# Clustered attention and two expert layers: a flag row for queries without keys, and one maximum over two PSUM banks in the first batch

## The chip, the core and the metric

One core of one Trainium2 chip. The metric is the device time of one execution in microseconds (us); the figure for a kernel is the median of its runs.

## The reference

Three stages follow each other. Attention: 2 batches, 8 heads, 768 positions, 64 columns. Each query and each key goes to the nearest of 16 centroids of its head, and a query sees only the keys of its own cluster:

```python
mask = q_assign[:, :, :, None] == k_assign[:, :, None, :]
scores = np.where(mask, scale * np.matmul(q, k.transpose(0, 1, 3, 2)), -1000000000.0)
attn = np.exp(scores - np.max(scores, axis=-1, keepdims=True))
attn = attn / (np.sum(attn, axis=-1, keepdims=True) + 1e-09)
return np.matmul(attn, v)
```

A query whose cluster holds no key has the same score everywhere, so its output is the mean of all values. The result, 1536 rows of 512, goes through a layer `s * relu(x @ w_in)**2 + b` times `w_out` (512 to 2048 to 512), and then through a layer of 8 experts of which each row uses the one with the largest gate.

## The kernel before, in words

A head is packed and transposed first (`prep1`, `prep2`). For each position `pk2` holds 128 columns in f16: 64 of the key (index 0) or the query (index 1), 16 of the one-hot cluster times a large number, then column 80, and zeros behind it. Column 80 is a constant on the key's side, and on the query's side it takes the query's negative maximum, so that a product of the packed rows gives a masked score with the maximum taken off. `prep2` also sums all values of the head in `vsp` (line 225) and keeps their mean in `vm` (line 227), on all partitions.

A unit is one head and one half of its queries: 3 chunks of 128, so that there are 32 units, 16 for each batch. `unit_max` (line 230) makes the maxima of a unit: for each chunk two matmuls of 384 keys into one PSUM bank each (line 239) and a reduce for each of the two (line 242), and behind the six a small reduce that joins the halves (line 248). The maxima go into column 80 (line 249), and the unit's packed queries are transposed into `qb`. After the second unit of a head an ACTIVATE makes a flag for each query whose maximum shows that it has no key (line 255).

`unit` (line 258) goes over 6 chunks of keys: two matmuls into `st` (lines 278 and 280), exponentials in f32 (`p`, line 283) and in half the cases in f16 too (`ph`, line 288, with the rest `pl` from POOL, line 291), and three chunks later their product with the values into `pv` (line 270), whose first column is the sum of the weights. Then VectorE makes the reciprocal and `x3` (lines 299 to 304), replaces the rows of flagged queries by `vm` with a COPY_PREDICATED (line 306), and ScalarE and POOL write `xp` in two parts (lines 309, 310).

The loop over heads runs `unit` of a head with `unit_max` of the next head, `prep2` of the one after that and `prep1` of the third laid in between, and from the ninth head on also steps of the second layer (`moe1`) for the first batch. Chunks of `w_in` and `w_out` are split into f16 pairs on the way (lines 324 to 333; 6 of them at the start, then in heads 5 and 7 to 11). This is the order of the program; within it a planner sets the order on each engine from a simulated timeline, and engines then run in order.

PSUM has eight banks. Before, two belong to `mm`, one to `aux`, two to `st`, two to `sm` and one to `pv`. In the first batch `mm` is free of the second layer, and the kernel uses it twice: for one of the six `sm` tiles of a unit, and for the `pv` of each second unit:

```python
sm = (mm.tile([P, HT], F32, name="sm", tag="mm") if n and c == 1 and i < H else
      sm_p.tile([P, HT], F32, name="sm"))
...
pv = (mm.tile([P, HC, D + 1], F32, name="pv", tag="mm") if i < H and qh else pv_p.tile([P, HC, D + 1], F32, name="pv"))
```

In the second batch all `pv` tiles come from the one bank of `pv_p`.

Of the kernel before, what the change touches and what calls it, by code (L numbers as in the profile page):

```python
# [26 lines left out]
BIGM = 32768.0  # L27
OOB = 1.0e6
# [15 lines left out]
def tile_kernel(ctx: ExitStack, tc, q, k, v, centroids, w_in, w_out, s, b, w_gate, w1, w2, out, dbg=None):  # L44
# [28 lines left out]
    mm = ctx.enter_context(tc.tile_pool(name="mm", bufs=2, space=PSUM))  # L73
# [7 lines left out]
    tpa = a0.enter_context(tc.tile_pool(name="tpa", bufs=4))  # L81
    at = ExitStack()
# [13 lines left out]
    sm_p = right("sm_p", 2, space=PSUM)  # L96
# [12 lines left out]
    def tpool(i):  # L109
        return tpa if i < H else tp  # L110

    def transpose(i, dst, src, pool=None):

        if i not in PE_T:
            nc.sync.dma_start_transpose(out=dst, in_=src.rearrange("p n x -> p (n x)"))
            return
        n0 = 2 * HC
        for g in range(0, src.shape[1], n0):
            nn = min(n0, src.shape[1] - g)
            odd = g // n0 % 2  # L120
            p, name = ((st_p, "st"), (sm_p, "sm"))[odd] if pool is None else pool
            ps = p.tile([P, n0, P], F16, name=name)
            for n in range(nn):
                nc.tensor.transpose(out=ps[:, n], in_=src[:, g + n], identity=ident)
            (nc.vector.tensor_copy if odd else nc.scalar.copy)(out=dst[:, g:g + nn], in_=ps[:, 0:nn])
# [34 lines left out]
    def iota(shape, pattern, base, mult, name):  # L160
# [10 lines left out]
    nc.gpsimd.memset(nokey, -BIGM * BIGM / 2)  # L171
# [5 lines left out]
                            compare_op=ALU.is_equal, fill=0.0)  # L177

# [6 lines left out]
    def pk2_clear(eng, i):  # L185
        eng.memset(pk2s[i][:, :, :, 64:128], 0.0)
        eng.memset(pk2s[i][:, 0, :, 64 + C], BIGM)

# [3 lines left out]
    def prep2(i):  # L192
# [33 lines left out]
        vm = tmp.tile([P, D], F32, name="vm", bufs=3)  # L226
        nc.scalar.activation(out=vm, in_=vsp, func=AF.Copy, scale=SX / S)
        h.update(pk2=pk2, tk2=tk2, qb={}, vm=vm)

    def unit_max(i, qh):  # L230
# [3 lines left out]
        mxt = small.tile([P, HC, 2], F32, name="mxt")  # L234
        for c in range(HC):
            for n in range(2):
                sm = (mm.tile([P, HT], F32, name="sm", tag="mm") if n and c == 1 and i < H else
                      sm_p.tile([P, HT], F32, name="sm"))
                nc.tensor.matmul(out=sm, lhsT=tk2[0:64 + C, 1, c0 + c, :],  # L239
                                 rhs=tk2[0:64 + C, 0, n * HC:(n + 1) * HC, :].rearrange("p c x -> p (c x)"),  # L240
                                 start=True, stop=True)
                nc.vector.tensor_reduce(out=mxt[:, c, n:n + 1], in_=sm, axis=AX.X, op=ALU.max)  # L242
                if (c, n) != (HC - 1, 1):
                    yield
        if not qh:
            h["mm1"] = small.tile([P, 2, HC], F32, name="mm1")
        mm1 = h["mm1"][:, qh]
        nc.vector.tensor_reduce(out=mm1, in_=mxt, axis=AX.X, op=ALU.max)
        st8[f"c{i}{qh}"] = nc.scalar.activation(out=pk2[:, 1, c0:c0 + HC, 64 + C], in_=mm1, func=AF.Copy, scale=-1.0 / BIGM)
        qb = tpool(i).tile([P, HC, P], F16, name="qb")  # L250
        transpose(i, qb, pk2[:, 1, c0:c0 + HC, :])
        h["qb"][qh] = qb
        if qh:
            h["flag"] = small.tile([P, 2, HC], F32, name="flag")
            nc.scalar.activation(out=h["flag"], in_=h["mm1"], func=AF.Relu, scale=-1.0, bias=nokey)
        yield

    def unit(i, qh, xp):
# [4 lines left out]
        pv = (mm.tile([P, HC, D + 1], F32, name="pv", tag="mm") if i < H and qh else pv_p.tile([P, HC, D + 1], F32, name="pv"))  # L263
# [12 lines left out]
        for kc in range(NC):  # L276
# [18 lines left out]
            yield  # L295
        for x in late:
            weigh(*x)
# [8 lines left out]
        nc.vector.copy_predicated(out=x3, mask=h["flag"][:, qh].bitcast(I32).unsqueeze(2).broadcast_to([P, HC, D]),  # L306
                                  data=h["vm"].unsqueeze(1).broadcast_to([P, HC, D]))
# [235 lines left out]
    for i in range(NH):  # L543
# [23 lines left out]
        if i == H - 1:  # L567
            a0.close()
            wop = ctx.enter_context(tc.tile_pool(name="wop", bufs=1, reuse_waits="tile"))
# [324 lines left out]
```

## Time and profile before

| | |
|---|---|
| median of 3 runs | 737.85 us (734.92 to 738.41) |
| the profiled execution's own time | 740.1 us |
| its span, first to last instruction | 738.4 us |
| mean granted clock of TensorE | 0.965 |
| busy: TensorE, VectorE, ScalarE, POOL | 89%, 71%, 59%, 40% |
| reduces of scores (line 242) | 192, mean 546 ns |
| COPY_PREDICATED (line 306) | 32, 21.8 us, mean 683 ns |
| products with the values (line 270), f16 | 1296, mean 195 ns |

A busy share is an average over stages: the first batch of attention ends at about 182 us, the second at about 415, the second layer at about 550, and the experts take the rest. Matmuls overlap in a pipeline, so the time from one's start to the next one's start is shorter than its duration; the same holds, by less, for VectorE.

### The profile page before, as it was taken

To read this page: it belongs to the slowest core of one execution; us is meant where nothing else is said; L and a number is where in the kernel's file an instruction comes from. 1 tells how busy PE (TensorE), PEld (TensorE's weight loads), DVE (VectorE), ACT (ScalarE), POOL (GpSimd) and SP (SyncE) were. 2 spreads that over 40 slices of the span, in tenths; PEclk is the share of its full clock that TensorE was granted. 3 is DMA by queue.
4 is the path that set the end of the run, shared out by engine and by line. 5 is a ranking of instruction groups with operands and counts; after the bars stand their busy time and mean duration, and the time that the engine had idled before them with its cause. 6 is when DMAs were issued, how large, how long until landed. Compare 5 with 4: busy or idle time off the path is not lost. (4 is left out here: it accounts for less than half of the span.)

```text
span 738.4 us, 16238 instructions
## 1 busy us (share of the span) xinstructions
PE 654.7 (89%) x6261; PEld 426.1 (58%) x6261; DVE 525.0 (71%) x1109; ACT 436.2 (59%) x897; POOL 293.5 (40%) x336
## 2 busy tenths in 40 slices
PE   2487888898877889999999999999999999998884
PEld 2255666676544545666655654565485776675651
DVE  7999798776899976588832661377844768777672
ACT  6477676777676745567734450156514568667562
POOL 6448576656666564644433300020013234331001
PEclk9998689999899999999999999999999999999898
DMA  8967666662563604430113400038933588789821
GB/s 235 185 158 154 146 169 145 154 133 54 141 158 95 150 25 99 107 70 7 34 13 67 85 15 1 15 110 260 373 101 100 127 270 270 163 270 255 258 101 52
DMA packets 122963, 98.33 MB, mean 133 GB/s; under 512 B 98812, under 2 KB 104956, under 8 KB 120576
## 3 DMA queue, kind: packets, MB, share of 16 engines
q1 hardware_dynamic: 112784, 65.64, 36.5%
q10 hardware_dynamic: 6576, 22.06, 9.4%
q0 software_dynamic: 3520, 9.54, 3.8%
q8 instruction: 51, 0.84, 0.5%
q14 instruction: 32, 0.26, 0.1%
HBM read 85.05 MB, written 7.39 MB: 125 GB/s over the span
## 5 line engine op out<-in xcount | busy, mean ns | idle before, releaser
L291 POOL TENSOR_TENSOR pl<-p,ph 128x384 f16<-128x384 f32 x128 | 128.4, 1011 | 116.4 <-ACT ph L288 58.7
L435 PE MATMUL ps<-xt,wi 128*128 128x384 f16 x768 | 135.3, 330 | 5.7 <-DMA xt<-xp 4.1
L449 PE MATMUL py<-wo,g 128*128 128x512 f16 x576 | 132.2, 382 | 0.0
L283 ACT ACTIVATE p<-st 128x384 f32<-128x384 f32 x192 | 94.1, 491 | 52.5 <-PE st L280 41.8
L242 DVE TENSOR_REDUCE mxt<-sm 128x1 f32<-128x384 f32 x192 | 102.3, 546 | 25.1 <-PE sm L239 24.5
L435 PEld LDWEIGHTS <-wi 128*128 128x128 f16 x768 | 74.5, 99 | 56.2 <-issue 10.4
L449 PEld LDWEIGHTS <-g 128*128 128x128 f16 x576 | 55.2, 98 | 64.0 <-issue 3.7
L239 PE MATMUL sm<-tk 80*128 80x384 f16 x192 | 64.5, 363 | 17.1 <-DVE mxt L242 11.9
L278 PE MATMUL st<-tk 128*128 128x384 f16 x192 | 65.6, 342 | 7.4 <-ACT ph L288 4.6
L288 ACT ACTIVATE ph<-st 128x384 f16<-128x384 f32 x144 | 70.9, 492 | 1.1 <-PE pv L270 1.1
L679 POOL DMA_INDIRECT out<-o,oid x16 | 26.9, 1682 | 103.4 <-ACT o L678 94.6
L280 PE MATMUL st<-qb,tk 128*128 128x384 f16 x192 | 65.8, 343 | 0.0
L673 PEld LDWEIGHTS <-ht 128*128 128x128 f16 x384 | 36.8, 98 | 44.5 <-issue 3.3
L441 ACT ACTIVATE g<-r,b 128x384 f16<-128x384 f32 x64 | 39.4, 618 | 37.1 <-DVE r L440 36.8
L442 DVE SCALAR_TENSOR_TENSOR g<-r,b,g 128x384 f16<-128x384 f32 x64 | 44.8, 701 | 21.3 <-ACT g L441 21.3
L270 PEld LDWEIGHTS <-ph 128*128 128x128 f16 x864 | 45.0, 99 | 20.9 <-issue 4.2
L270 PE MATMUL pv<-v,ph 128*128 128x65 f16 x864 | 52.0, 195 | 5.4 <-ACT ph L288 3.2
L516 POOL DMA_INDIRECT yreg<-yp,posi x12 | 12.8, 1069 | 106.6 <-DVE posi L502 86.1
L599 DVE SCALAR_TENSOR_TENSOR wa<-stg,wa 128x1024 f16<-128x1024 f32 x40 | 46.8, 1218 | 7.7 <-ACT wa L598 7.6
L659 PE MATMUL hps<-x2t,wa 128*128 128x128 f16 x768 | 45.7, 219 | 3.8 <-DVE wa L599 1.5
L659 PEld LDWEIGHTS <-wa 128*128 128x128 f16 x768 | 43.7, 98 | 6.8 <-issue 2.0
L440 DVE SCALAR_TENSOR_TENSOR r<-r,s 128x384 f32<-128x384 f32 x64 | 43.4, 678 | 4.2 <-ACT r L438 4.0
(216 smaller groups left out, 1248.0 us busy)
## 6 DMA issues: line engine op xcount, KB each, us to landing
stg<-in_moe_w SPq DMA_DIRECT2D x44, 1024.0 KB
raw<-in_moe_w_out ACTq DMA_DIRECT2D x16, 512.0 KB
stg<-in_moe_w ACTq DMA_DIRECT2D x8, 1024.0 KB
raw<-in_moe_w_in ACTq DMA_DIRECT2D x10, 512.0 KB
kqv<-in_k SPq DMA_DIRECT2D x16, 192.0 KB
kqv<-in_q SPq DMA_DIRECT2D x16, 192.0 KB
kqv<-in_v SPq DMA_DIRECT2D x16, 192.0 KB
raw<-in_moe_w_in SPq DMA_DIRECT2D x6, 512.0 KB
```

Of the source, the lines that this page charges most:

```text
L239: nc.tensor.matmul(out=sm, lhsT=tk2[0:64 + C, 1, c0 + c, :], rhs=tk2[0:64 + C, 0, n * HC:(n + 1) * HC, :].rearrange("p c x -> p (c x)"), s ...
L242: nc.vector.tensor_reduce(out=mxt[:, c, n:n + 1], in_=sm, axis=AX.X, op=ALU.max)
L270: nc.tensor.matmul(out=pv[:, c, :], lhsT=p[:, c * P:(c + 1) * P], rhs=w, start=first[0], stop=(kc == NC - 1 and c == HC - 1 and p is parts ...
L278: nc.tensor.matmul(out=st.rearrange("p (c x) -> p c x", c=HC), lhsT=tk1[:, kc, 0, :], rhs=tk1[:, c0:c0 + HC, 1, :], start=True, stop=False)
L280: nc.tensor.matmul(out=st, lhsT=tk2[:, 0, kc, :], rhs=qb.rearrange("p c x -> p (c x)"), start=False, stop=True)
L283: nc.scalar.activation(out=p32, in_=st, func=AF.Exp, scale=1.0 / 8.0)
L288: nc.scalar.activation(out=ph, in_=st, func=AF.Exp, scale=1.0 / 8.0)
L291: eng.tensor_tensor(out=pl, in0=p32, in1=ph, op=ALU.subtract)
L435: nc.tensor.matmul(out=ps, lhsT=wi[:, a, kk, f * P:(f + 1) * P], rhs=xt[:, c, kk], start=(kk == 0 and n == 0), stop=(kk == KD - 1 and n == 2))
L449: st8["py"] = nc.tensor.matmul(out=ps, lhsT=g[:, a, f, c * P:(c + 1) * P], rhs=wo[:, w, f], start=(f == 0 and n == 0), stop=(f == KF - 1 a ...
L599: nc.vector.scalar_tensor_tensor(out=lo[:, a:z], in0=stg[i][:, a:z], scalar=SW, in1=hi[:, a:z], op0=ALU.mult, op1=ALU.subtract)
L659: nc.tensor.matmul(out=ps[:, j], lhsT=ws[:, w, kk * F + f0:kk * F + f0 + P], rhs=xt[:, a, kk], start=(i == 0), stop=(i == 3 * KD - 1))
```

## The change

It makes four connected edits. First, in `pk2` column 96 becomes a flag row: on the key's side the constant -65504, on the query's side the output of an ACTIVATE (Relu of the maximum, scaled) which is zero for a query with keys; it is written before `qb` is transposed, once for each unit. A flagged query's scores then fall to where the exponential is zero. Second, `vm` is a tile of 128 partitions, zero but for partition 96, which holds 768 and the sum of the values, in two f16 parts; three such tiles are kept and written by an ACTIVATE and a subtract of one partition for each head. Six matmuls for each unit (two for each of three chunks) add flag times that row to `pv`, so that a flagged query gets sum over 768. The COPY_PREDICATED and the old flag go. Third, up to the ninth head the two matmuls of a chunk write the two banks of one tile of `smw`, and one reduce goes over both; the small reduce behind goes there. Fourth, the banks for this come from `mm` and `sm_p`, which are opened only when the first batch is over; until then `pv` has one bank.

```diff
@@ -25,6 +25,8 @@
 SY = 4.0
 SW = 64.0
 BIGM = 32768.0
+LOST = -65504.0
+FL = 96
 OOB = 1.0e6
 
 
@@ -70,7 +72,6 @@
     dram = ctx.enter_context(tc.tile_pool(name="dram", bufs=1, space=DRAM))
     small = ctx.enter_context(tc.tile_pool(name="small", bufs=3))
     ypool = ctx.enter_context(tc.tile_pool(name="ypool", bufs=2))
-    mm = ctx.enter_context(tc.tile_pool(name="mm", bufs=2, space=PSUM))
     aux = ctx.enter_context(tc.tile_pool(name="aux", bufs=1, space=PSUM))
 
     yreg = dram.tile([E * N, ROW // 2], I32, name="yreg")
@@ -79,6 +80,7 @@
 
     a0 = ExitStack()
     tpa = a0.enter_context(tc.tile_pool(name="tpa", bufs=4))
+    smw = a0.enter_context(tc.tile_pool(name="smw", bufs=2, space=PSUM))
     at = ExitStack()
 
     def right(name, bufs, **kw):
@@ -93,7 +95,6 @@
     tmp = right("tmp", 2)
     fw = right("fw", 2)
     st_p = right("st_p", 2, space=PSUM)
-    sm_p = right("sm_p", 2, space=PSUM)
     pv_p = right("pv_p", 1, space=PSUM)
 
     cpool = ExitStack()
@@ -118,8 +119,8 @@
         for g in range(0, src.shape[1], n0):
             nn = min(n0, src.shape[1] - g)
             odd = g // n0 % 2
-            p, name = ((st_p, "st"), (sm_p, "sm"))[odd] if pool is None else pool
-            ps = p.tile([P, n0, P], F16, name=name)
+            p, name = ((st_p, "st"), (smw, "sm"))[odd] if pool is None else pool
+            ps = p.tile([P, 2, 8, P], F16, name=name)[:, 0] if p is smw else p.tile([P, n0, P], F16, name=name)
             for n in range(nn):
                 nc.tensor.transpose(out=ps[:, n], in_=src[:, g + n], identity=ident)
             (nc.vector.tensor_copy if odd else nc.scalar.copy)(out=dst[:, g:g + nn], in_=ps[:, 0:nn])
@@ -168,13 +169,15 @@
     wt_c = const.tile([P, C], F16, name="wt_c")
     nc.vector.tensor_copy(out=wt_c, in_=wt32)
     nokey = const.tile([P, 1], F32, name="nokey")
-    nc.gpsimd.memset(nokey, -BIGM * BIGM / 2)
+    nc.gpsimd.memset(nokey, -1.0)
     ones16 = const.tile([P, P], F16, name="ones16")
     nc.gpsimd.memset(ones16, 1.0)
 
     ident = const.tile([P, P], F16, name="ident")
     nc.gpsimd.affine_select(out=ident, in_=ones16, pattern=[[1, P]], base=0, channel_multiplier=-1,
                             compare_op=ALU.is_equal, fill=0.0)
...
     pk2s = []
@@ -185,6 +188,14 @@
     def pk2_clear(eng, i):
         eng.memset(pk2s[i][:, :, :, 64:128], 0.0)
         eng.memset(pk2s[i][:, 0, :, 64 + C], BIGM)
+        eng.memset(pk2s[i][:, 0, :, FL], LOST)
+
+    vms = []
+    for i in range(3):
+        t = const.tile([P, 2, D + 1], F16, name=f"vms{i}")
+        nc.gpsimd.memset(t, 0.0)
+        nc.gpsimd.memset(t[FL:FL + 1, 0, 0:1], float(S))
+        vms.append(t)
 
     def pk2_of(i):
         return pk2s[i % 4] if i < H else pk2s[i % 2]
@@ -223,36 +234,38 @@
         for c in range(NC):
             for t in range(2):
                 nc.tensor.matmul(out=vsp, lhsT=ones16, rhs=v1[:, c, t, 1:1 + D], start=(c == 0 and t == 0), stop=(c == NC - 1 and t == 1))
-        vm = tmp.tile([P, D], F32, name="vm", bufs=3)
-        nc.scalar.activation(out=vm, in_=vsp, func=AF.Copy, scale=SX / S)
+        vm = vms[i % 3]
+        nc.scalar.copy(out=vm[FL:FL + 1, 0, 1:1 + D], in_=vsp[FL:FL + 1])
+        nc.vector.tensor_tensor(out=vm[FL:FL + 1, 1, 1:1 + D], in0=vsp[FL:FL + 1], in1=vm[FL:FL + 1, 0, 1:1 + D], op=ALU.subtract)
         h.update(pk2=pk2, tk2=tk2, qb={}, vm=vm)
 
     def unit_max(i, qh):
         h = hd[i]
         pk2, tk2 = h["pk2"], h["tk2"]
         c0 = qh * HC
-        mxt = small.tile([P, HC, 2], F32, name="mxt")
+        mm1 = small.tile([P, HC], F32, name="mm1")
+        mxt = None if i <= H else small.tile([P, HC, 2], F32, name="mxt")
         for c in range(HC):
+
+            sm = smw.tile([P, 2, 512], F32, name="sm") if i <= H else None
             for n in range(2):
-                sm = (mm.tile([P, HT], F32, name="sm", tag="mm") if n and c == 1 and i < H else
-                      sm_p.tile([P, HT], F32, name="sm"))
-                nc.tensor.matmul(out=sm, lhsT=tk2[0:64 + C, 1, c0 + c, :],
+                part = sm[:, n, 0:HT] if i <= H else sm_p.tile([P, HT], F32, name="sm")
+                nc.tensor.matmul(out=part, lhsT=tk2[0:64 + C, 1, c0 + c, :],
                                  rhs=tk2[0:64 + C, 0, n * HC:(n + 1) * HC, :].rearrange("p c x -> p (c x)"),
                                  start=True, stop=True)
-                nc.vector.tensor_reduce(out=mxt[:, c, n:n + 1], in_=sm, axis=AX.X, op=ALU.max)
+                if i > H:
+                    nc.vector.tensor_reduce(out=mxt[:, c, n:n + 1], in_=part, axis=AX.X, op=ALU.max)
+                elif n:
+                    nc.vector.tensor_reduce(out=mm1[:, c:c + 1], in_=sm[:, :, 0:HT], axis=AX.XY, op=ALU.max)
                 if (c, n) != (HC - 1, 1):
                     yield
-        if not qh:
-            h["mm1"] = small.tile([P, 2, HC], F32, name="mm1")
-        mm1 = h["mm1"][:, qh]
-        nc.vector.tensor_reduce(out=mm1, in_=mxt, axis=AX.X, op=ALU.max)
+        if i > H:
+            nc.vector.tensor_reduce(out=mm1, in_=mxt, axis=AX.X, op=ALU.max)
         st8[f"c{i}{qh}"] = nc.scalar.activation(out=pk2[:, 1, c0:c0 + HC, 64 + C], in_=mm1, func=AF.Copy, scale=-1.0 / BIGM)
+        nc.scalar.activation(out=pk2[:, 1, c0:c0 + HC, FL], in_=mm1, func=AF.Relu, scale=-2.0 / BIGM ** 2, bias=nokey)
         qb = tpool(i).tile([P, HC, P], F16, name="qb")
         transpose(i, qb, pk2[:, 1, c0:c0 + HC, :])
         h["qb"][qh] = qb
-        if qh:
-            h["flag"] = small.tile([P, 2, HC], F32, name="flag")
-            nc.scalar.activation(out=h["flag"], in_=h["mm1"], func=AF.Relu, scale=-1.0, bias=nokey)
         yield
 
     def unit(i, qh, xp):
@@ -260,7 +273,7 @@
         h = hd[i]
         tk1, tk2, v1, qb = h["tk1"], h["tk2"], h["v1"], h["qb"][qh]
         c0 = qh * HC
-        pv = (mm.tile([P, HC, D + 1], F32, name="pv", tag="mm") if i < H and qh else pv_p.tile([P, HC, D + 1], F32, name="pv"))
+        pv = pv_p.tile([P, HC, D + 1], F32, name="pv")
 
         def weigh(kc, parts):
             first = [kc == 0]
@@ -293,6 +306,9 @@
             if kc >= LAG:
                 weigh(*late.pop(0))
             yield
+        for c in range(HC):
+            for n in range(2):
+                nc.tensor.matmul(out=pv[:, c, :], lhsT=qb[:, c, :], rhs=h["vm"][:, n], start=False, stop=False, skip_group_check=True)
         for x in late:
             weigh(*x)
         den = small.tile([P, HC], F32, name="den")
@@ -303,8 +319,6 @@
         x3 = tmp.tile([P, HC, D], F32, name="x3")
         nc.vector.tensor_tensor(out=x3, in0=pv[:, :, 1:1 + D], in1=rec.unsqueeze(2).broadcast_to([P, HC, D]),
                                 op=ALU.mult)
-        nc.vector.copy_predicated(out=x3, mask=h["flag"][:, qh].bitcast(I32).unsqueeze(2).broadcast_to([P, HC, D]),
-                                  data=h["vm"].unsqueeze(1).broadcast_to([P, HC, D]))
         kk, o = divmod(hh * D, P)
         nc.scalar.copy(out=xp[:, qh, 0, kk, :, o:o + D], in_=x3)
         nc.gpsimd.tensor_tensor(out=xp[:, qh, 1, kk, :, o:o + D], in0=x3, in1=xp[:, qh, 0, kk, :, o:o + D],
@@ -566,6 +580,8 @@
             load(i + 4)
         if i == H - 1:
             a0.close()
+            mm = ctx.enter_context(tc.tile_pool(name="mm", bufs=2, space=PSUM, reuse_waits="tile"))
+            sm_p = right("sm_p", 2, space=PSUM, reuse_waits="tile")
             wop = ctx.enter_context(tc.tile_pool(name="wop", bufs=1, reuse_waits="tile"))
             gpool = act.enter_context(tc.tile_pool(name="gpool", bufs=1, reuse_waits="tile"))
             xtpool = act.enter_context(tc.tile_pool(name="xtpool", bufs=2, reuse_waits="tile"))
```

## Rows read from the trace of the kernel before

**Rows 1.** Windows: length, busy us of each engine (xinstructions), clock, DMA, GB/s

```profile
41.00:70.00 29.00, 23.64 (x195) 16.11 (x194) 27.64 (x53) 21.86 (x52) 20.13 (x21) 0.97 0.71 165
100.00:122.00 22.00, 18.98 (x220) 14.22 (x218) 21.36 (x49) 16.74 (x45) 13.77 (x19) 1.00 0.74 171
122.00:182.00 60.00, 54.41 (x651) 41.69 (x650) 43.46 (x114) 44.03 (x121) 36.66 (x42) 0.97 0.52 112
200.00:266.00 66.00, 53.17 (x517) 32.29 (x514) 64.53 (x108) 46.09 (x107) 41.92 (x38) 0.97 0.44 118
266.00:415.00 149.00, 145.84 (x1429) 87.55 (x1427) 90.47 (x246) 86.20 (x220) 66.93 (x86) 0.99 0.27 55
```

**Rows 2.** Windows, the stretch at the lower clock (same columns)

```profile
70.00:84.00 14.00, 13.37 (x103) 9.97 (x103) 9.38 (x25) 9.33 (x24) 6.08 (x7) 0.50 0.50 116
```

**Rows 3.** Timeline of PE, 64 to 71 us: start, us, what, xcount [idle before]

```profile
67.49 0.33 PE L280 MATMUL st<-qb,tk 128*128 128x384 f16 x1
69.36 0.48 PE L239 MATMUL sm<-tk 80*128 80x384 f16 x1 [1.54 <-DVE mxt L242]
```

**Rows 4.** Timeline of DVE, 64 to 71 us (same columns)

```profile
65.13 1.00 DVE L242 TENSOR_REDUCE mxt<-sm 128x1 f32<-128x384 f32 x2
66.06 1.79 DVE L330 SCALAR_TENSOR_TENSOR m<-raw,l 128x512 uint32<-128x512 uint32 x1
67.78 1.07 DVE L306 COPY_PREDICATED x<-flag,vm 128x192 f32<-128x192 int32 x1
68.76 1.01 DVE L242 TENSOR_REDUCE mxt<-sm 128x1 f32<-128x384 f32 x2
```

**Rows 5.** Groups by line, whole run: xcount, busy us, mean ns, idle before

```profile
L208 DVE TENSOR_REDUCE mx<-sim 128x12 f32<-128x192 f32 x16 | 5.6, 347 | 4.5 <-PE sim L204 4.5
...
L248 DVE TENSOR_REDUCE mm<-mxt 128x3 f32<-128x6 f32 x32 | 4.8, 149 | 0.2
...
L255 ACT ACTIVATE flag<-mm,nokey 128x6 f32<-128x6 f32 x16 | 4.7, 294 | 0.0
...
L145 POOL MEMSET v<- 128x6 f16 x16 | 1.8, 122 | 3.8 <-PE pv L270 3.8
```

**Rows 6.** Groups of DVE, 24 to 41 us

```profile
L242 DVE TENSOR_REDUCE mxt<-sm 128x1 f32<-128x384 f32 x16 | 8.5, 546 | 0.6 <-PE sm L239 0.6
```

**Rows 7.** Groups of DVE, 41 to 70 us

```profile
L242 DVE TENSOR_REDUCE mxt<-sm 128x1 f32<-128x384 f32 x22 | 11.6, 542 | 1.1 <-PE sm L239 1.1
...
L306 DVE COPY_PREDICATED x<-flag,vm 128x192 f32<-128x192 int32 x2 | 2.2, 1077 | 0.0
```

**Rows 8.** Groups of DVE, 100 to 122 us

```profile
L242 DVE TENSOR_REDUCE mxt<-sm 128x1 f32<-128x384 f32 x21 | 10.9, 542 | 0.1
...
L306 DVE COPY_PREDICATED x<-flag,vm 128x192 f32<-128x192 int32 x2 | 1.4, 720 | 0.0
```

**Rows 9.** Groups of DVE, 200 to 266 us

```profile
L306 DVE COPY_PREDICATED x<-flag,vm 128x192 f32<-128x192 int32 x3 | 2.3, 754 | 0.0
```

**Rows 10.** Timeline of PE, 116.7 to 117.05 us: six matmuls of 65 columns

```profile
116.80 0.35 PE L270 MATMUL pv<-v,ph 128*128 128x65 f16 x6
116.99 0.32 PE L278 MATMUL st<-tk 128*128 128x384 f16 x1
```

**Rows 11.** Timeline, 161 to 163.2 us: between two units of the first batch

```profile
161.71 0.25 PE L270 MATMUL pv<-v,pl 128*128 128x65 f16 x3
...
161.80 0.86 PE L270 MATMUL pv<-vw,p 128*128 128x65 f32 x6
...
162.50 0.49 PE L239 MATMUL sm<-tk 80*128 80x384 f16 x2
...
162.68 0.36 DVE L304 TENSOR_TENSOR x<-pv,rec 128x192 f32<-128x192 f32 x1
```

**Rows 12.** Waits of PE, 182 to 300 us: us in total, times, longest us

```profile
PE pv L270 <- DVE x L304: 2.1, 1, 2.1
```

**Rows 13.** Waits of PE, 41 to 182 us (same columns)

```profile
PE sm L239 <- DVE mxt L242: 5.8, 8, 1.7
```

## The prediction

> **What bounds the kernel now.** I read the table of windows first, by stage, then VectorE's groups in the stages where it is full, then the timeline around the places where TensorE stops, and last the waits. The stages are not bound by the same engine [rows 1]. At 41 to 70, 100 to 122 and 200 to 266 us VectorE is busy 27.64 of 29, 21.36 of 22 and 64.53 of 66 us: it is the bound there. From 266 to 415 us TensorE is busy 145.84 of 149. From 70 to 84 the granted clock is 0.50, the 1.2 GHz level, with TensorE busy 13.37 of 14 [rows 2]: half speed is the bound there. From 122 to 182 TensorE is the fullest, 54.41 of 60, but not full. So an instruction taken from VectorE pays in the first three stretches (117 us together), an instruction given to TensorE costs from 266 on and wherever its clock is low.
>
> The fall of the clock has a visible history. TensorE ends a matmul that began at 67.49, waits 1.54 us for a maximum and starts the next at 69.36, now 0.48 us long where it was 0.33 [rows 3]. The reduce that it waits for starts at 68.76, right behind a COPY_PREDICATED that ran from 67.78 for 1.07 us [rows 4]: one of the instructions that this change removes.
>
> **The change, part by part.** The sum is made against the profiled execution: 740.1 us, of which the span is 738.4. The median shown is 737.85, so 2.25 us come off at the end.
>
> *Wide maximum.* Two reduces of 384 become one of 768, up to the ninth head. Two in a row start at 65.13 and the next instruction at 66.06 [rows 4], so a pair takes 0.93, or 0.465 each. A reduce of 192 elements takes 347 ns and one of 384 takes 546 [rows 5, 6]: 1.04 ns an element, so 768 should take 546 + 398 = 944 ns, less the 80 ns by which neighbours overlap (546 - 465): 0.86. A pair saves 0.07 us. From 24 to 122 us there are 16 + 22 + 21 = 59 reduces where it counts [rows 6 to 8], or 29.5 pairs: -2.1. The small reduce behind each six goes too, 149 ns less the 80 of overlap [rows 5], some 10 times: -0.7.
>
> For this price the Trainium skill (VectorE: DVE Perf Modes, The TRN2 errata) has a fixed 120 cycles for each PSUM source, an estimate of 125 ns. By it the pairs save 3.7 us and the sum comes out 1.6 lower; the trace's 0.07 decides.
>
> *COPY_PREDICATED goes.* In the three full stretches: two at 1.077, two at 0.720, three at 0.754 us [rows 7 to 9], each less 0.08 of overlap: 2.0 + 1.3 + 2.0 = -5.3. The other 25 lie where VectorE has gaps: nothing. At one place, the end of the first batch, it also stands between x3 and the transposed activations that TensorE awaits; I take -0.5, between nothing and its longest mean, 1.08.
>
> *New on VectorE:* a subtract on one partition for each head, 64 elements. No row shows it; the nearest are a small reduce at 0.07 and a full 192-element one at 0.347 less 0.08, or 0.27 [rows 5]. I take 0.1, near the small one, for about 8 heads prepared in full stretches: +0.8.
>
> VectorE thus gets 8.1 - 0.8 = 7.3 us back where it is full. TensorE is itself busy 23.64 of 29 and 53.17 of 66 there [rows 1], so what is late next is TensorE, and ScalarE with 21.86 and 46.09. I take two thirds, **-5.0**; ends 0 and -7.3.
>
> *Six matmuls for each unit* (128 x 128 by 65 columns, twice for each of three chunks). Six such start at 116.80 and the next matmul at 116.99 [rows 10]: 0.19 us at 2.4 GHz, so some 0.38 at 1.2. Of 32 units some 12 end after 266 us: +2.3 in full. Three lie at half clock: +1.1. Eight at 122 to 182, of which half fits into gaps: +0.8. The rest lie under VectorE. **+4.2**; ends 2.3 and 32 x 0.19 + 0.6 = 6.7.
>
> *One bank for pv in the first batch.* Before, units alternate between two. The row of a boundary: the old unit's last product starts at 161.71, the next unit's first at 161.80, though x3 reads the old bank only from 162.68 for 0.36 [rows 11]. With one bank the next unit's products wait until 163.04, 1.24 us later, and behind them in TensorE's order wait the scores of the unit. TensorE can pull other work forward, as the pair for a maximum at 162.50, which fills the 0.3 us to x3, and about as much again of scores: some 0.6 stay. Where VectorE is full this is hidden, unless x3 itself stands late in its queue. Eleven boundaries lie outside, eight of them at 122 to 182; the gaps of 5.6 us there absorb part: 0.2 each, **+2.2**; ends 0 and 15 x 1.24 = 18.6. In the second batch there is one bank already, and there TensorE waited on x3 once, 2.1 us [rows 12], with much other work at hand.
>
> *The flag moves ahead of the transpose:* an ACTIVATE now stands before each qb transpose, 0.29 us [rows 5]. Only the first unit waits for it directly: +0.3. Later ones are made a unit ahead, and the transposes on SP's queue just start that much later, as many as before. ScalarE gets 16 more of these, +4.7 us over the run, hidden at 59% busy (without that cover, 4.7). Memsets at the launch, about six at 122 ns [rows 5], lie on POOL beside the first load: nothing, at most 0.7. The three vm buffers add a wait of ScalarE's copy on the matmuls of three heads back, long done: nothing; if late, the exponentials queue behind it.
>
> Sum: -5.0 - 0.5 + 4.2 + 2.2 + 0.3 = +1.2, so 741.3 for the profile, **739** for the median. That is within 0.5% (3.7 us), about what a measurement of this kernel can tell from no change.
>
> **Rivals.** *The single bank rules* (slower). Mechanism: each unit's weighted sum waits for reciprocal and x3 of the one before. It decides once x3 ends more than some 0.65 us behind the last product, what TensorE can pull forward. For: the row has 1.24, on a stretch where VectorE was free. Against: in the second batch it cost one wait. Price: the full 1.24 at the eleven boundaries is 13.6 instead of 2.2, so 739 + 11.4 = 750; falls of the clock would come on top. Its rule stands in the Trainium skill (Perfetto Trace Analysis, Optimizing Tensor Performance): independent groups should rotate through different banks, so that reading one overlaps the next one's matmuls. The alternation at 161.71 and 161.80 agrees with it.
>
> *The clock stays up* (faster). Mechanism: without the copy at 67.78 the maximum comes about 1 us earlier, the wait of 1.54 shrinks to some 0.5, and the four half-banks for maxima let TensorE run further ahead of VectorE; such waits are 5.8 us in 8 [rows 13]. TensorE's 13.37 busy us from 70 to 84 then take half, -6.7, and VectorE's relief comes whole, -2.3: 739 - 9 = 730. Against: from 60 to 70 VectorE is short of time anyway, and waits on x3 may let the clock fall elsewhere.
>
> *The wide maximum does not pay*: reading over two banks costs as much as two reads. Then 2.1 stay on VectorE; two thirds of it is 1.4, 740.4.
>
> **How the numbers follow.** Forecast 0.34, single bank 0.29, clock 0.32, no gain from width 0.05. The forecast's own range, from the bounds of its terms near the chosen values, is 734 to 744: it gives 0.26 to the same, 0.05 to faster and 0.03 to slower. So faster 0.37, same 0.31, slower 0.32. Both signs are open, hence the range is wide: down to the clock rival with the full six-matmul cover hidden (730 - 4 = 726), up to the bank rival with one short fall of the clock (750 + 2 = 752).
>
> **What would show it.** Right: L242 in the first batch in half the number at about 0.94 us; no COPY_PREDICATED; six more matmuls of 65 columns for each unit at 0.19; the stretch to the first batch's end within some 2 us of 182; about 2.5 us more from there to 415, less what VectorE gives back at 200 to 266. The bank rival is right if the waits show pv held by x3 around ten times at over half a us in the first batch. The clock rival is right if the clock row of 70 to 84 is 1.00. Wrong altogether: if the order that the planner makes differs so much that the stages cannot be laid side by side, or if the time changes after 550 us.

## The result, and the profile after

The changed kernel is slower by about 1%. Its median is 748.43 us against 737.37 for the kernel before in the same runs, a ratio of 1.0112 (95% interval 1.0064 to 1.016). The ratios here and below compare fast runs alone (of the four of the changed kernel 758.96 us was a slow one), so they are not the quotients of the medians. The forecast was 739, within 0.5%, with a range of 726 to 752; the rival with the single bank stood at 750. The profiled execution is the fastest of those measured: 743.3 us, span 741.6, 5.1 us under the median. So what its trace shows is the loss at its smallest.

The windows of the changed kernel, with the columns of [rows 1] (70 to 84 us answers to [rows 2], the others to [rows 1]):

```profile
41.00:70.00 29.00, 24.77 (x254) 17.98 (x253) 27.00 (x43) 21.48 (x54) 20.12 (x22) 0.88 0.73 176
70.00:84.00 14.00, 10.12 (x72) 7.43 (x72) 11.82 (x20) 10.21 (x28) 9.06 (x12) 0.77 0.72 168
100.00:122.00 22.00, 20.09 (x246) 16.30 (x246) 15.34 (x30) 14.51 (x38) 11.40 (x18) 0.89 0.62 152
122.00:182.00 60.00, 52.39 (x646) 40.23 (x644) 34.76 (x78) 42.21 (x116) 33.48 (x38) 0.97 0.45 104
200.00:266.00 66.00, 52.72 (x506) 31.71 (x505) 65.70 (x105) 48.03 (x109) 41.49 (x38) 0.92 0.48 125
266.00:415.00 149.00, 144.29 (x1501) 88.49 (x1501) 89.21 (x241) 86.61 (x229) 69.05 (x86) 1.00 0.27 52
```

VectorE did get its relief: 15.34 us of 22 where it had 21.36, and 34.76 of 60 where it had 43.46. The clock at 70 to 84 us rose from 0.50 to 0.77. Neither is paid out: from 100 to 122 the clock fell from 1.00 to 0.89, and TensorE is busy 52.39 of 60 us at 122 to 182 where it was 54.41.

The groups of the new instructions (line, engine, tiles, count | busy, mean ns | idle before, releaser):

```profile
L259 DVE TENSOR_REDUCE mm<-sm 128x1 f32<-128x768 f32 x54 | 50.3, 945 | 8.2 <-PE sm L253 8.1
L311 PE MATMUL pv<-vms,qb 128*128 128x65 f16 x192 | 12.1, 197 | 0.0
L265 ACT ACTIVATE pk<-mm,nokey 128x3 f16<-128x3 f32 x32 | 9.6, 299 | 0.0
L239 DVE TENSOR_TENSOR vms<-vsp,vms 1x64 f16<-1x64 f32 x16 | 3.7, 231 | 12.3 <-ACT vms L238 12.0
```

The wide reduction takes 945 ns (944 was worked out). The subtract on one partition takes 231 ns, not the 0.1 us taken for it, and VectorE stands idle 12.3 us ahead of the sixteen of them, nearly all behind ScalarE. The waits of the changed kernel, TensorE's at 41 to 182 us and the largest of VectorE's at 41 to 185 us (total, times, longest):

```profile
PE st L291 <- ACT ph L301: 5.4, 8, 1.0
PE sm L253 <- DVE mm L259: 5.1, 5, 1.3
PE pv L283 <- ACT ph L301: 3.0, 3, 1.7
...
PE pv L283 <- DVE x L320: 1.8, 2, 1.1
...
DVE vms L239 <- ACT vms L238: 10.1, 5, 4.4
DVE den L315 <- PE pv L283: 8.7, 7, 2.5
```

Of the wait that the bank rival named, pv for x3, there are only two, 1.8 us. So the waits by name do not show where the time went. The times of x3 do. It ends each unit, so the starts of the first and the sixteenth x3 bound the first batch:

| | first x3 | sixteenth x3 | between | from there to the end |
|---|---|---|---|---|
| before | 57.9 | 181.75 | 123.8 | 556.6 |
| after | 53.7 | 184.35 | 130.6 | 557.2 |

The batch starts 4.2 us earlier and takes 6.8 longer. What follows it differs by 0.6.

What happens between two units is seen best at the fifth x3. VectorE of the changed kernel, around it (start, us, line):

```profile
94.47 0.94 DVE L259 TENSOR_REDUCE mm<-sm 128x1 f32<-128x768 f32 x1
95.33 0.14 DVE L315 TENSOR_SCALAR den<-pv 128x3 f32<-128x3 f32 x1
95.40 0.94 DVE L259 TENSOR_REDUCE mm<-sm 128x1 f32<-128x768 f32 x1
96.27 0.67 DVE L344 SCALAR_TENSOR_TENSOR m<-raw,l 128x512 uint32<-128x512 uint32 x1
96.86 0.16 DVE L318 RECIPROCAL rec<-den 128x3 f32<-128x3 f32 x1
96.97 0.43 DVE L340 TENSOR_SCALAR l<-raw 128x512 uint32<-128x512 uint32 x1
97.32 0.35 DVE L320 TENSOR_TENSOR x<-pv,rec 128x192 f32<-128x192 f32 x1
```

and TensorE (the last products of the old unit are those at 90.26, the next unit's first those at 97.98):

```profile
90.26 0.26 PE L283 MATMUL pv<-v,pl 128*128 128x65 f16 x3
...
93.46 0.32 PE L291 MATMUL st<-tk 128*128 128x384 f16 x1
93.62 0.33 PE L293 MATMUL st<-qb,tk 128*128 128x384 f16 x1
94.58 0.48 PE L291 MATMUL st<-tk 128*128 128x384 f16 x1 [0.64 <-ACT ph L301]
94.86 0.52 PE L293 MATMUL st<-qb,tk 128*128 128x384 f16 x1
96.01 0.48 PE L291 MATMUL st<-tk 128*128 128x384 f16 x1 [0.63 <-ACT p L296]
96.28 0.52 PE L293 MATMUL st<-qb,tk 128*128 128x384 f16 x1
97.39 0.48 PE L291 MATMUL st<-tk 128*128 128x384 f16 x1 [0.58 <-ACT ph L301]
97.66 0.53 PE L293 MATMUL st<-qb,tk 128*128 128x384 f16 x1
97.98 1.38 PE L283 MATMUL pv<-vw,p 128*128 128x65 f32 x6
```

The old unit's products are done at 90.5. VectorE has no gap there. It reaches den at 95.33 and x3 at 97.32; between the two stand a reduction and two steps of a weight chunk. For 7 us no product of the next unit can run. The planner has put its scores forward instead, and these go at the pace of the exponentials: a pair each 1.4 us, with a gap of some 0.6 before each. Behind the first of these gaps the clock is lower: the granted clock is 1.00 from 90 to 94.3 us and 0.50 from 94.5 to 98.5, and the same matmul takes 0.32 us at 93.46 and 0.48 at 94.58. The products that were left over then run at the lower clock from 97.98 on. So at this place the loss appears as short waits of the scores for ScalarE, and as clock, while what the products wait for is the bank.

Over the fifteen boundaries of the first batch in this trace, the time from the old unit's last product to den sums to 12.3 us, and from den to the end of x3 to 27.9: 2.7 us a boundary. The first five hold 26.1 of the 40.2. At all fifteen the next unit's first product starts only when x3 has ended: 50.8 us in sum behind the old unit's last product, 3.4 each. In the kernel before, the next unit's first product starts ahead of the old unit's end, by 16.3 us in sum.

### The profile page after: what moved, and what is told of

The parts are those of the page before. It is cut to its first block, busy times and chain, and to the rows that moved or that the text cites. A ratio compares the mean times of both kernels' runs of the same rounds, so it can differ in the third digit from the quotient of the medians.

```text
span 741.6 us, 16537 instructions
## 1 busy us (share of the span) xinstructions
PE 655.9 (88%) x6453; PEld 430.3 (58%) x6453; DVE 513.5 (69%) x1023; ACT 442.4 (60%) x913; POOL 284.1 (38%) x344
## 4 chain that ended last, share of the span: by engine, by line
PE 46%; DMA 17%; DVE 15%; issue 13%; ACT 5%; POOL 2%; SPq 1%; POOLq 0%; ACTq 0%; DVEq 0%
PE py L463 15%; PE ps L449 12%; DMA out<-o,oid 7%; PE pv L283 6%; DMA tk<-pk 3%; PE hps L675 3%; DVE l L341 2%; PE st L291 2%; PE sm L253 2%; PE st L293 2%; DMA raw<-in_moe_w_in 2%; DVE l L340 2%; DMA kqv<-in_q 2%; DVE mm L259 2%; DVE m L344 2%
## 5 line engine op out<-in xcount | busy, mean ns | idle before, releaser
L304 POOL TENSOR_TENSOR pl<-p,ph 128x384 f16<-128x384 f32 x128 | 125.9, 989 | 117.6 <-ACT ph L301 47.1
L449 PE MATMUL ps<-xt,wi 128*128 128x384 f16 x768 | 138.2, 330 | 2.3 <-DMA xt<-xp 1.8
L253 PE MATMUL sm<-tk 80*128 80x384 f16 x192 | 55.9, 359 | 19.9 <-DVE mxt L257 7.4
L695 POOL DMA_INDIRECT out<-o,oid x16 | 19.9, 1245 | 109.0 <-ACT o L694 94.0
L283 PE MATMUL pv<-v,ph 128*128 128x65 f16 x864 | 54.3, 197 | 4.0 <-ACT ph L301 3.0
L530 POOL DMA_INDIRECT yreg<-yp,posi x12 | 12.7, 1061 | 116.8 <-DVE posi L516 90.1
L257 DVE TENSOR_REDUCE mxt<-sm 128x1 f32<-128x384 f32 x84 | 44.6, 549 | 18.5 <-PE sm L253 17.1
L259 DVE TENSOR_REDUCE mm<-sm 128x1 f32<-128x768 f32 x54 | 50.3, 945 | 8.2 <-PE sm L253 8.1
```

What stands on the lines that cost most here:

```text
L253: nc.tensor.matmul(out=part, lhsT=tk2[0:64 + C, 1, c0 + c, :], rhs=tk2[0:64 + C, 0, n * HC:(n + 1) * HC, :].rearrange("p c x -> p (c x)"), ...
L259: nc.vector.tensor_reduce(out=mm1[:, c:c + 1], in_=sm[:, :, 0:HT], axis=AX.XY, op=ALU.max)
L283: nc.tensor.matmul(out=pv[:, c, :], lhsT=p[:, c * P:(c + 1) * P], rhs=w, start=first[0], stop=(kc == NC - 1 and c == HC - 1 and p is parts ...
L304: eng.tensor_tensor(out=pl, in0=p32, in1=ph, op=ALU.subtract)
L449: nc.tensor.matmul(out=ps, lhsT=wi[:, a, kk, f * P:(f + 1) * P], rhs=xt[:, c, kk], start=(kk == 0 and n == 0), stop=(kk == KD - 1 and n == 2))
```

## Experiments

Each run is compared with the kernel before on the same chip; before had medians of 739.36 (e1 to e4), 739.65 (e5 to e8) and 739.41 us (e9 to e12). Theory A: the single pv bank is what costs. Theory B: the six matmuls. Theory C: the chain of waits behind the vm buffer. First the outcome of all, with the times read from each one's single profiled execution as above:

| kernel | median us | ratio to before, 95% interval | first x3 | first to sixteenth | rest |
|---|---|---|---|---|---|
| **one pv bank** | | | | | |
| after | 748.43 | 1.0112 (1.0064 to 1.016) | 53.7 | 130.6 | 557.2 |
| e1 one bank alone | 750.08 | 1.0124 (1.0074 to 1.0174) | 60.2 | 140.1 | 556.2 |
| e3 wide maximum alone | 748.97 | 1.0117 (1.0069 to 1.0165) | 52.6 | 135.0 | 559.7 |
| e4 vm copy on VectorE | 755.41 | 1.0223 (1.0165 to 1.0282) | 56.7 | 138.9 | 554.6 |
| e6 five vm buffers | 759.28 | 1.0234 (1.0174 to 1.0295) | 56.1 | 143.9 | 557.2 |
| e7 after, early copy | 744.06 | 1.0070 (1.0035 to 1.0104) | 56.1 | 124.3 | 559.6 |
| e10 e1, early copy | 750.91 | 1.0155 (1.0097 to 1.0212) | 59.5 | 131.7 | 555.5 |
| **two pv banks** | | | | | |
| before | | 1 | 57.9 | 123.8 | 556.6 |
| e2 flag row alone | 736.52 | 0.9943 (0.9903 to 0.9983) | 56.75 | 121.6 | 556.6 |
| e5 after, second bank | 747.1 | 1.0093 (1.0055 to 1.0131) | 66.9 | 117.9 | 561.3 |
| e8 e2, wide for head 0 | 738.49 | 1.0028 (0.9987 to 1.0069) | 56.1 | 120.7 | 558.6 |
| e9 e2, no six matmuls | 735.82 | 0.9988 (0.995 to 1.0026) | 56.3 | 120.4 | 556.0 |
| e11 e2, early copy | 744.12 | 1.0080 (1.004 to 1.0119) | 59.8 | 121.0 | 559.7 |
| e12 before, five vm | 744.34 | 1.0067 (1.0028 to 1.0106) | 57.5 | 126.5 | 557.7 |

(The profiled execution of e1 is 8 us above its median, so its 140.1 is too long.)

**e1: the bank alone**

```diff
-        pv = (mm.tile([P, HC, D + 1], F32, name="pv", tag="mm") if i < H and qh else pv_p.tile([P, HC, D + 1], F32, name="pv"))
+        pv = pv_p.tile([P, HC, D + 1], F32, name="pv")
```

> The kernel before, with the pv tile of every unit from the one bank of pv_p; nothing else. Theory A (the single pv bank costs the time: units of the first batch wait for x3): 745 to 751 us, and the waits of TensorE show pv held by x3 for 5 us or more in the first batch. Theory B (the six matmuls for each unit cost it, on a full TensorE) and theory C (the new vm chain costs it: ScalarE's copy waits for the matmuls that still read the vm buffer, and VectorE's subtract waits for ScalarE): 735 to 740, as before.

750.08 against 739.36: +10.7 us by this line alone, with nothing else of the change in it. The time is where theory A had it; its other sign, 5 us or more of waits of pv for x3, was not met (3.5 us in six waits): as in after, the waits by name do not show the loss.

**e2: the flag row alone**, on the banks of before: the change without its hunks on `smw`, `mm`, `sm_p`, the reductions and `pv`. Its core against before:

```diff
+        nc.scalar.activation(out=pk2[:, 1, c0:c0 + HC, FL], in_=mm1, func=AF.Relu, scale=-2.0 / BIGM ** 2, bias=nokey)
...
+        for c in range(HC):
+            for n in range(2):
+                nc.tensor.matmul(out=pv[:, c, :], lhsT=qb[:, c, :], rhs=h["vm"][:, n], start=False, stop=False, skip_group_check=True)
...
-        nc.vector.copy_predicated(out=x3, mask=h["flag"][:, qh].bitcast(I32).unsqueeze(2).broadcast_to([P, HC, D]),
-                                  data=h["vm"].unsqueeze(1).broadcast_to([P, HC, D]))
```

> The flag row alone on the old PSUM layout: two pv banks in the first batch, two reduces of 384 for a chunk. Theory A: 732 to 738, since VectorE is freed of the COPY_PREDICATED and no unit waits for x3. Theory B: 740 to 744 (six matmuls at 0.19 us for 32 units, half of them on a full TensorE, less what VectorE gains). Theory C: 744 to 749, with VectorE waiting for ScalarE at the subtract of vm for 8 us or more in the first batch.

736.52, the only kernel whose interval lies below the kernel before. The flag row does not cost the loss, and with it theories B and C fall.

**e3: the wide maximum alone**, with the banks that it brings: the other hunks. Its core against before:

```diff
+    smw = a0.enter_context(tc.tile_pool(name="smw", bufs=2, space=PSUM))
...
+                    nc.vector.tensor_reduce(out=mm1[:, c:c + 1], in_=sm[:, :, 0:HT], axis=AX.XY, op=ALU.max)
...
+        pv = pv_p.tile([P, HC, D + 1], F32, name="pv")
```

> The wide maximum alone, with its PSUM layout (one pv bank until the ninth head) and the old flag and COPY_PREDICATED. Theory A: 744 to 750. Theories B and C: 733 to 738, a little under before for the reduces saved.

748.97, as e1 and after. The first x3 comes at 52.6, 5.3 us earlier, and the stretch behind it takes that back and 6 us more. (The early first x3 does not come with every wide maximum: e4, e6 and e7 have one too, and theirs is at 56.1 to 56.7.)

**e4: vm's first part copied by VectorE**

```diff
-        nc.scalar.copy(out=vm[FL:FL + 1, 0, 1:1 + D], in_=vsp[FL:FL + 1])
+        nc.vector.tensor_copy(out=vm[FL:FL + 1, 0, 1:1 + D], in_=vsp[FL:FL + 1])
```

> The changed kernel, with the first part of vm copied by VectorE instead of ScalarE, so that the subtract behind it waits for no other engine. Theory C: 741 to 745, since VectorE no longer stands behind ScalarE's queue; what is left is the wait for the matmuls that read the buffer. Theories A and B: 746 to 750, as the changed kernel.

755.41, slower still, and above all the expected ranges. VectorE now stands itself behind the matmuls that read the old vm; of its waits at 41 to 185 us:

```profile
DVE vms L238 <- PE pv L311: 9.1, 4, 2.6
```

**e5: the second bank back**, for one of the two wide buffers

```diff
-    smw = a0.enter_context(tc.tile_pool(name="smw", bufs=2, space=PSUM))
+    smw = a0.enter_context(tc.tile_pool(name="smw", bufs=1, space=PSUM))
+    pvw = a0.enter_context(tc.tile_pool(name="pvw", bufs=1, space=PSUM))
...
-        pv = pv_p.tile([P, HC, D + 1], F32, name="pv")
+        pv = (pvw if i < H and qh else pv_p).tile([P, HC, D + 1], F32, name="pv")
```

> The changed kernel with a second pv bank for the odd chunks of the first batch, paid for with one of the two wide score buffers. Theory A (the one pv bank costs 9 to 11 us): the boundaries come free again and the run goes to 738 to 742, some 8 us under the changed kernel's 748.4, with no wait of pv for x3 above 1 us in 41 to 182 us. Rival D (the wide reduction itself, or any PSUM layout with wide scores, is what costs): no more than 2 us come back, 746 or above. A third case, both: the waits of pv go, but TensorE now waits for the single wide buffer at each second query tile (0.95 us a reduction), and the run stays at 744 to 750 with waits of sm for mm in place of those of pv.

The third case. The stretch of sixteen units fell to 117.9 us, the shortest of all, 12.7 under after. But the first x3 came 13.2 us later. VectorE of e5:

```profile
43.36 0.69 DVE L345 SCALAR_TENSOR_TENSOR m<-raw,l 128x512 uint32<-128x512 uint32 x1
49.55 0.43 DVE L341 TENSOR_SCALAR l<-raw 128x512 uint32<-128x512 uint32 x1 [5.50 <-DMA raw<-in_moe_w_in]
49.89 0.95 DVE L260 TENSOR_REDUCE mm<-sm 128x1 f32<-128x768 f32 x1
```

In this order a step of a weight chunk stands ahead of the reduction, 5.5 us before its data is there, and again at 57.99 (5.23). With one wide buffer TensorE waits for such a reduction up to 4.5 us, 10.8 us in seven waits. That the single buffer caused the order of the chunks is not shown.

**e6: five vm buffers**

```diff
-    for i in range(3):
+    for i in range(5):
...
-        vm = vms[i % 3]
+        vm = vms[i % 5]
```

> The changed kernel with five buffers for the mean of the values in place of three. Theory A (the pv bank alone costs, and the waits of ScalarE and VectorE behind the mean's buffer are its consequence): ScalarE's wait for the mean's matmuls (4.9 us in 41 to 185 us) goes, the time stays at 746 to 750. Rival C2 (the chain of VectorE behind ScalarE behind the mean's matmuls adds to the loss by itself): 3 to 5 us come back, 743 to 745.

759.28. Neither theory has this: the edit takes a wait away and the time rises by 11 us against after. ScalarE's wait for the old vm's readers is gone. The planner made another order, and in it TensorE's clock is lower. Window 41 to 182 us of after:

```profile
41.00:182.00 141.00, 120.09 (x1347) 91.31 (x1345) 104.64 (x192) 101.25 (x264) 85.53 (x98) 0.90 0.57 138
```

and of e6:

```profile
41.00:182.00 141.00, 120.31 (x1193) 91.53 (x1190) 104.32 (x183) 91.23 (x235) 77.84 (x87) 0.79 0.61 141
```

TensorE is as busy, and gets through 1193 matmuls where it was 1347. So each edit counts as two: its resource, and a new order.

**e7: pv copied out at once**

```diff
         den = small.tile([P, HC], F32, name="den")
+        pvs = tmp.tile([P, HC, D + 1], F32, name="pvs")
+        nc.vector.tensor_copy(out=pvs, in_=pv)
...
```

(den and x3 read `pvs` for `pv`.)

> The changed kernel with pv copied out of its bank in one VectorE instruction, the three steps after it reading the copy. Theory A1 (the bank is held by the length of the chain den, rec, x3): the bank comes free 0.3 to 0.4 us earlier at each of 15 boundaries, while the copy adds some 0.3 us of VectorE to each of 32 chunks; 743 to 746. Rival A2 (the bank is held because VectorE reaches den late, behind waits and reductions of its own queue): the copy comes as late as den came, no gain, and the added work makes it 748 to 753.

744.06, within A1's range. The stretch is 6.3 us shorter than in after. The groups of e7 show what it costs (den took 154 ns from the bank):

```profile
L315 DVE COPY pvs<-pv 128x195 f32<-128x195 f32 x32 | 11.3, 353 | 22.4 <-PE pv L283 22.3
L317 DVE TENSOR_SCALAR den<-pvs 128x3 f32<-128x3 f32 x32 | 11.0, 343 | 0.3
```

From the first reader to the last the bank is now held 5.2 us in fifteen boundaries, where it was 27.9. But the copy itself comes late: 22.3 us from last product to first reader over the fifteen boundaries, where it was 12.3 (the 22.3 in the row above is another sum, VectorE's idle time ahead of all 32 copies). So the hold went from 40.2 to 27.5, and A2 has a share in it.

**e8: wide maximum for the first head alone**, whose scores are reduced before pv is needed (on the flag row of e2; the lines are against e2)

```diff
-                sm = (mm.tile([P, HT], F32, name="sm", tag="mm") if n and c == 1 and i < H else
+                sm = (wide[:, n, 0:HT] if not i else mm.tile([P, HT], F32, name="sm", tag="mm") if n and c == 1 and i < H else
...
     run(unit_max(0, 1))
+    w0.close()
+    mm = ctx.enter_context(tc.tile_pool(name="mm", bufs=2, space=PSUM, reuse_waits="tile"))
```

> The flag row on the PSUM layout of the kernel before, with the wide maximum for the first head alone, whose scores are reduced before any pv bank is needed; the wide buffers are given up before the other heads start. Theory A (the wide maximum is worth what it brought to the first unit, some 4 us, once it takes no pv bank): the first x3 comes at 53 to 54 us in place of 57.9, and the time is 732 to 736, at or under the 736.5 of the flag row alone. Rival E (what comes earlier at the first unit is given back before the end of the first batch, because the loads set its pace): the first x3 is earlier, the time stays at 736 to 738.

738.49, just over the range of rival E. The first x3 moved by 0.6 us only, not by the 3 to 4 expected, so the earlier first unit of after and e3 does not come from the first head's maxima alone; what brings it is not shown.

**e9: e2 without the six matmuls**

```diff
-        for c in range(HC):
-            for n in range(2):
-                nc.tensor.matmul(out=pv[:, c, :], lhsT=qb[:, c, :], rhs=h["vm"][:, n], start=False, stop=False, skip_group_check=True)
```

> The flag row on the two-bank layout (e2, 736.5) without the six matmuls of each chunk that add the mean of the values; it leaves out the output of queries without keys. By the prediction's price of the six, 0.19 us a chunk at full clock: 732 to 733, most of the gain after the first chunk of the second batch. Rival I (they fit into idle time of TensorE): 735 to 738.

735.82, rival I. By ratio it is no better than e2 (0.9988, 0.9943); by medians it is 0.7 us better (735.82, 736.52), by profiled spans 2.2 (732.7, 734.9).

**e10: e1 with the early copy** (the diff of e7, on e1)

> The kernel before with one pv bank for all chunks (e1, 750.1) and pv copied out of it by one VectorE instruction. Theory A1 (what costs is how long the bank is held after the last product, 0.8 to 5 us a chunk from the first reader to the last, because the order puts other VectorE work between den, rec and x3): the hold falls to one copy of some 0.35 us and the run comes back to 740 to 745, with neither flag row nor wide maximum in it. Rival F (the order that the planner finds for any one-bank layout is slow, however long the bank is held): it stays at 747 to 753.

750.91: rival F; A1 fails here. The hold after the last product is 23.4 us in fifteen boundaries (18.2 up to the copy, 5.2 in it), half of e1's 46.7 and less than in e7, and the run is not faster than e1.

**e11: e2 with the early copy** (the diff of e7, on e2)

> The flag row on the two-bank layout (e2, 736.5) with the same copy. Theory A1: with two banks the next chunk does not need the bank that is being read, so the copy frees nothing that is waited for and only adds some 0.3 us of VectorE to each chunk: 736 to 741. Rival G (the copy gains by itself, in any layout): 731 to 734, and then the gain of e7 says nothing of the bank.

744.12, slower than e2, and above A1's range (736 to 741) too: G falls, the copy gains nothing by itself. With e10 it is a pair that differs in the bank and the flag row: 131.7 against 121.0 us for the stretch.

**e12: an edit without a resource in it**

```diff
-        vm = tmp.tile([P, D], F32, name="vm", bufs=3)
+        vm = tmp.tile([P, D], F32, name="vm", bufs=5)
```

> The kernel before with five buffers in place of three for the mean of the values, which no trace shows it waiting for; the planner lays out a different order all the same. It measures how far the order alone moves the time. Theory A: the two-bank layouts stay together whatever the order, 735 to 742, well apart from the 748 to 759 of the one-bank kernels. Rival H (the spread of the orders is as large as the difference that was put down to the bank): 745 or more, or 730 or less.

744.34, between A's range and H's: another order alone moves the kernel before by 0.67%. A difference of this size between two kernels here can be their order; e2's gain of 0.6% is no larger.

**What the runs settle.** The rest after the sixteenth x3 is 554.6 to 561.3 us in all fourteen kernels, so most of what differs lies ahead of it. Without a copy the stretch from first to sixteenth x3 is 130.6 to 143.9 us with one bank (five kernels) and 117.9 to 126.5 with two (six): no overlap. e1, the one line, gives +10.7 us by medians; the two pairs that differ in the bank and the wide maximum give +9.0 (after, e2) and +11.2 us (e3, before) in the stretch. With the copy the groups are nearer, 124.3 and 131.7 against 121.0. The wait for the bank is seen in each trace: from a unit's last product to the next unit's first, the fifteen boundaries sum to 50.6 to 63.1 us in the five kernels with one bank, and to 33.0 and 30.3 in the two with the copy, while in the seven kernels with two banks the next unit starts ahead of that end, by 10.2 to 20.2 us in sum. The clock is the other part, and not the same in each: over the stretch it is 0.81 to 0.86 in e3, e4 and e6, but 0.91 in after, where before has 0.89.

**Shown** is that the line that leaves pv one bank makes this kernel slower, by about 10 us, and that nothing else in the change is needed for that. **Open** is how it splits between the hold itself and the order that the planner finds around it: e7 and e10 disagree, each layout had few orders, and an order can move a kernel by as much (e6 lies 10.9 us above after, with the same bank). No order was held fixed while the bank changed; that was not tried.

## Why the prediction was right in its range and wrong in its sum

The result lies inside the range of 726 to 752, since that ran up to the single-bank rival, which had a chance of 0.29; the sum itself, 739, is 9.4 us too low. That its small sign, +1.2 us on the profile, is the measured one is luck: it is what was left of a relief of 5.5 and costs of 6.7.

**The step that failed is "One bank for pv".** It was +2.2 with ends 0 and 18.6; e1 and the pairs measure 9 to 11. The mechanism stood there as the rival at 750, and the runs put after at 748.43. Three things in the step were wrong.

First, the row of the boundary was misread [rows 11]. The products at 161.71 and 161.80 are both of the next unit, its second and third chunk of keys. Counted from the first unit on, the old unit's last products and the next one's first stand here:

```profile
159.30 0.78 PE L270 MATMUL pv<-vw,p 128*128 128x65 f32 x6
160.41 0.25 PE L270 MATMUL pv<-v,pl 128*128 128x65 f16 x3
...
162.22 0.14 DVE L299 TENSOR_SCALAR den<-pv 128x3 f32<-128x3 f32 x1
```

The next unit starts at 159.30, before the old one's last products, which end at 160.66; den comes 1.56 us behind them, and x3 ends at 163.04. So one bank puts the next unit's first product back by 3.74 us here, and not by 1.24. Since the rival's price is made of the same 1.24, that its 750 came so near is in part luck.

Second, this was one place, where VectorE ran den, rec and x3 almost together. The kernel before shows otherwise at its third unit:

```profile
74.97 0.15 DVE L299 TENSOR_SCALAR den<-pv 128x3 f32<-128x3 f32 x1
...
77.14 0.17 DVE L302 RECIPROCAL rec<-den 128x3 f32<-128x3 f32 x1
...
78.59 0.35 DVE L304 TENSOR_TENSOR x<-pv,rec 128x192 f32<-128x192 f32 x1
```

3.97 us from den to the end of x3. Over fifteen units it was 32.5 us before, 2.2 each, and 0.8 only at the shortest; from the last product on, 49.7. With two banks no product waited for that, so no wait pointed at it.

Third, "Where VectorE is full this is hidden, unless x3 itself stands late in its queue". The condition was the rule. In the kernel before, the time from the last product to the end of x3 is 5.2 us on average at the four boundaries at 41 to 70 and 100 to 122 us, which were priced at nothing, and 2.6 at the other eleven. Against e2, the first four boundaries of after, up to the fifth x3, take 43.6 us in place of 39.1: 4.5 of the 9.0. Two of these were priced at nothing, two at 0.2. The other 4.6 lie on eleven boundaries, 0.4 each. From unit to unit the difference goes both ways (-3.3 to +7.4 us), so this split is rough. The point from which the rival decides, x3 ending 0.65 us behind the last product, was passed in the trace of after at every boundary (0.86 at the least).

The rule of the Trainium skill that was set beside this rival (Perfetto Trace Analysis, Optimizing Tensor Performance), that independent groups should rotate through different banks, is borne out here: the one line of e1 costs 10.7 us. (The two rows named beside it, 161.71 and 161.80, are of one unit and one bank; the alternation is at 159.30 and 160.41.)

The other steps:

- *Wide maximum.* The duration was right, 945 ns. A pair saves 0.06 us where 0.07 was taken, and e1 against e3 (750.08, 748.97) shows no gain that can be told from none. The first x3 at 52.6 to 53.7 us was not forecast. The Trainium skill's fixed price for a PSUM source (VectorE: DVE Perf Modes, The TRN2 errata) would have given more: the trace has 28.61 to 29.48 us from a wide reduction's start to the next instruction's, 0.87, against 0.93 for a pair before [rows 4], so 0.06 is saved and not the estimated 0.125. (That estimate would have lowered the sum by 1.1, not by the 1.6 named, since two thirds of VectorE's relief were counted.)
- *COPY_PREDICATED goes, VectorE's relief.* The direction was right: in e2, which has it with two banks, the stretch is 2.2 us shorter than before and the clock over 41 to 182 us is 0.94, where it was 0.90. The size, 5 us, can't be told from what an order moves (e12).
- *Six matmuls*, +4.2. They take 197 ns each, 12.1 us busy. Their worth by e9 is 2.2 us by spans, 0.7 by medians and nothing by ratio; 4.2 was too much if anything.
- *The clock stays up.* Its sign was not met: 0.77 at 70 to 84 us. It gave less than the rival's 6.7, and falls of the clock elsewhere took it back.
- *The vm buffers*, "long done: nothing". In after it was not so: VectorE stood 10.1 us behind ScalarE's copy, ScalarE 4.9 us behind the matmuls that read the old vm. It goes with the late products: in e2 the same wait of VectorE is 0.2 us at 41 to 185 us, and taking the buffer's limit away (e6) brought nothing.
- *A planner's new order* was named as what would make the prediction wrong altogether. It did not hide the stages, but it is worth 0.7% in e12, more than the 0.5% on which the chances were built.

## What to carry to other kernels

When a change takes away a second buffer, sum up over all uses in the old trace how long each buffer stays held after its last write, the readers' queue included; an overlap that works leaves no wait to find. Count the instructions to be sure which unit a row belongs to. Look at the stage where the reading engine is full: there the hold was longest in this case, not hidden. Where a planner lays out the order, run an edit without effect as well, and call no difference a gain that is smaller than what that moves.

## What the runs showed of the hardware that was not expected

- den and x3 take longer from the copy in SBUF than from the bank: 343 ns against 154, and 510 against 351 (e7 and after), behind a copy of 353. These durations overlap with their neighbours. From start to the next instruction's start, where VectorE does not idle between, the medians are 0.27 us for the copy, 0.20 in place of 0.11 for den, and 0.27 in both kernels for x3.
- A subtract on one partition and 64 elements takes 231 ns. x3, 192 elements on all 128 partitions, takes 351; at the 1.04 ns an element of the reductions, 64 of them would take an estimated 218. By this estimate the 127 partitions not used save nothing.
- Gaps of 0.58 to 0.64 us between pairs of matmuls, as at 94.58 to 97.39 us in after, go with the lower level of TensorE's clock, 1.2 GHz: the matmul takes 0.48 us there and 0.32 ahead of them. No single one of them stands out in the waits, and the six products behind them still take 1.38 us.
